# Parameter loads on ScalarE's queue, the first half of x in ten loads, and a new order of a fused S4 convolution and GEGLU kernel

## Chip, cores and metric

One core of a Trainium2 chip. The metric is device time in microseconds of one execution of the whole kernel; the table below also has the span from a profiled execution, from its first to its last instruction.

## What is computed

Two branches read the same input x (2048 tokens, 640 channels) and a gate mixes them: a causal convolution of every channel with a kernel K built from 128 complex modes, and a feed-forward layer of width 1728 with a GELU gate. Everything comes in and goes out as bfloat16.

```python
g  = sigmoid((x * gate_w).sum(-1, keepdims=True))
dt = exp(log_dt)[:, None];  logdA = dt * (A_re + 1j*A_im);  dB = dt * (B_re + 1j*B_im)
K  = einsum("dn,dnl,dn->dl", C_re + 1j*C_im, exp(logdA[:, :, None] * arange(2048)), dB).real
a  = irfft(rfft(pad(x)) * rfft(pad(K)))[:2048] + x * Dskip      # over time, per channel
b  = (gelu(x @ w_gate) * (x @ w_up)) @ w_down                    # 640 -> 1728 -> 640
out = g * a + (1 - g) * b
```

## The kernel before

The program is a set of named steps (`step(name, fn)`), each of which issues a few instructions on one engine, and a text, ORDER, that lists the names in the order in which they are emitted. Every engine runs its instructions in that order, and so does each queue of DMAs; semaphores make an instruction wait for what it reads and for what still uses the place it writes. A suffix in ORDER gives a product's PSUM tile (`/0` to `/3`) or the engine of an eviction (`/A` ScalarE, `/D` VectorE). The DMAs of SP and ScalarE share eight semaphores in turn (DMAHW0 to DMAHW7 in the rows below): a DMA is only issued when the last one with its semaphore has landed.

The work goes in stages.

- *Loads.* `lp0` to `lp5` load the six parameter arrays, `lpk` a constant with identity matrices, `ldt` the step sizes, `lw0` the first block of gate and up weights in two DMAs (line 277, 278), `x0.0` to `x4.0` the first 1024 tokens of x, one transposing DMA of 128 channels each (line 285). `t0` to `t5` turn the parameters on TensorE (line 302), `dt` is ScalarE's first exponential (line 322), `c2`, `c3` copies (331), `al`, `th`, `v0` to `v18` small vector arithmetic.
- *Tables.* For each half h of the channels, `xa`, `xb` are exponentials (ScalarE), `fb`, `fa` phase chunks (VectorE, lines 481 and 474), `qb`, `qa` the quarter turn, `sb`, `sa` sines (lines 490 and 484), `ma`, `pa`, `pb`, `pc` table products (VectorE); `pa6.h` is the last. `ct{h}.0` to `.6` then contract the tables to K on TensorE, and `ek{h}.0` to `.6` evict it. The second half's exponentials overwrite the tables, so they wait for the contraction of the first.
- *Gate and up products.* `g{ft}.{th}`, `u{ft}.{th}` multiply 128 columns of weights by 1024 tokens of half th (two blocks of 512 tokens, five matmuls each, line 381); `eg`, `eu` evict them. They stand between the table steps. `h.{th}` holds the last 64 columns of both, and is evicted in two instructions of 64 rows. Up values and the second half's gate values go through a ring of three buffers to DRAM and come back later (`su`, `sg`, `rl`, `rg`, `hm`).
- *Spectra.* `U` and `K` are matmuls with cosine and sine matrices (lines 706, 719), evicted by `eU`, `eK`. `gl` computes the gate in 80 matmuls of one column (line 625).
- *Products and output.* For half h and block c of 512 frequencies, `m{h}{c}{i}{part}` multiplies spectrum i of x with spectrum c - i of K (lines 761, 764), `s...` adds it to the sum (765), `y{h}{c}0/1` close it (767, 768), all on VectorE; `I` transforms back (779), `D` is the down projection (794, 28 matmuls each), `Z` adds the convolution through a permutation (801, 802), `o` and `st` scale, evict and store.

One buffer holds each product of `m` until its `s` has added it:

```python
step(f"m{h}{c}{i}{part}", lambda ux=ux, kx=kx: tt(out=fl(t), in0=ux, in1=kx, op=ALU.mult))
step(f"s{h}{c}{i}{part}", lambda dst=dst, op=op: tt(out=fl(dst), in0=fl(dst), in1=fl(t), op=op))
```

Of the kernel before, what the change touches and what calls it, by code (L numbers as in the profile page):

```python
# [40 lines left out]
lp0 lpk ldt idx one tdt/0 tabE dt oa.0 sk leu2 lp5 lw0 lp3 t0/1 al xb23.0 xa4.0 xb6.0 xa10.0 al2 xa5.0 xa17.0 lp4 x0.0  # L41
lp2 t4/2 t2/3 xb4.0 xa19.0 c2 xb9.0 xb14.0 x1.0 t5/0 x4.0 x3.0 lp1 t3/1 c3 x2.0 v0 v3 ur0 ob.0 xa9.0 xb17.0 xb2.0
xb1.0 xb13.0 xa1.0 xa3.0 v1 v5 v2 t1/3 ul0 th v4 xb12.0 v6 v7 xb5.0 xa8.0 xb8.0 fb0.0 fb1.0 qb0.0 g1.0/1 eg1.0/D v8
uf0.1 v11 uf0.0 u1.0/2 xb21.0 xb11.0 v9 xa16.0 xb15.0 v10 xa11.0 xb3.0 xb27.0 xa14.0 eu1.0/D g0.0/0 u0.0/3 eu0.0/A v12
v13 v14 mag xb31.0 v15 xa7.0 xb7.0 xb29.0 xb25.0 xb19.0 xb10.0 xa15.0 v16 tabT sb0.0 x4.1 lw1 qb1.0 eg0.0/D g3.0/1
# [5 lines left out]
sa1.0 eg9.0/A fa3.0 sa2.0 pa1.0 u10.0/1 eu10.0/A qa3.0 sa3.0 pa2.0 u9.0/2 eu9.0/A fa4.0 qa4.0 pa3.0 fa5.0 sa4.0 fa6.0
qa5.0 pa4.0 qa6.0 eu8.0/A g11.0/0 u12.0/1 u11.0/2 eg11.0/A sa5.0 ma5.0 fil.0 pa5.0 g10.0/3 su8.0 su9.0 lu00 lw7 leu0
h.0/0 sa6.0 pa6.0 eu12.0/A eg10.0/D ct0.4/1 ek0.4/D eu11.0/A ct0.0/2 ct0.6/3 ek0.6/D uf2.0 uf2.1 ct0.3/1 ek0.0/A
eg13.0/A ct0.2/2 ct0.1/3 ek0.1/D ek0.3/A su10.0 su12.0 su11.0 ct0.5/1 ek0.2/D ek0.5/D ur3 oa.1 ob.1 u12.1/3 tabE2
xb8.1 fil.1 eu12.1/D ks.0 xa7.1 xb29.1 xb27.1 xb9.1 xa1.1 xb13.1 ma0.1 xa8.1 xb3.1 xa9.1 xa10.1 xb4.1 xa14.1 xb19.1
# [5 lines left out]
fb4.1 pc2.1 qb4.1 U002/0 eU002/A sb3.1 eg2.1/A sb4.1 u4.1/1 U001/0 eU001/A eu4.1/A su2.1 lfm3 g4.1/2 eg4.1/A pc3.1
fb5.1 pb3.1 fa0.1 pc4.1 qb5.1 qa0.1 pb4.1 lw11 sg2.1 lka2 kt.0 sg4.1 eu3.1/A sb5.1 lka0 su4.1 su3.1 u5.1/0 U003/1
eU003/A fa1.1 pb5.1 qa1.1 sa0.1 eu5.1/A sa1.1 g5.1/2 g7.1/3 K002/1 g6.1/0 fa2.1 pa0.1 qa2.1 eg5.1/A fa3.1 pa1.1 qa3.1
sa2.1 eg6.1/A sa3.1 pa2.1 fa4.1 fa5.1 qa4.1 qa5.1 pa3.1 u6.1/2 gl/0 lw12 lfm0 sg5.1 su5.1 lka1 sg6.1 eu6.1/A su6.1
eK002/A lwd0 rl0.0 U000/2 eU000/D eg7.1/A sa4.1 u7.1/3 K003/2 fa6.1 pa4.1 qa6.1 sa5.1 gl1 eu7.1/A eK003/A sa6.1 K001/0
# [812 lines left out]
```

## Time and profile before

| | |
|---|---|
| time, median of 3 runs | 290.39 us (289.47, 290.39, 292.72) |
| profiled execution, span | 287.8 us; no other time of it is given |
| busy, PE / VectorE / ScalarE | 264.4 / 261.7 / 221.0 us |
| DMA | 46.94 MB, mean 163 GB/s |

Durations below are from the profiled execution. Busy time of an engine leaves out register, semaphore and DMA-issuing instructions; overlapping instructions of one engine are counted once, and a group's mean is that of one instruction from its issue to its end, so that two back to back take less than twice the mean. DVE is VectorE, ACT ScalarE, PE TensorE, PEld its weight loads; SPq and ACTq are the DMA issues on the queues of SP and ScalarE. The digits of PEclk are the clock granted to TensorE in 40 equal slices, in tenths of full speed.

### The profile page before, as it was taken

How to read it: one execution, taken by the hardware profiler on the slowest of the kernel's cores; microseconds unless marked ns; L12 is line 12 of the kernel's file. 1: busy time of each engine (PE TensorE's matmuls, PEld its weight loads, DVE VectorE, ACT ScalarE, POOL GpSimd, SP SyncE). 2: the span in 40 equal slices, each digit the busy share in tenths (PEclk: the TensorE clock that was granted, in tenths of full speed). 3: DMA queues.
4: the chain of work that ended last, by engine and by line, in shares of the span. 5: the costliest groups of instructions: out<-in, count | busy, mean ns of one | idle time of the engine just before them, and what ended most of it. 6: DMA issues, size and time to landing. Idle time of an engine off the chain costs nothing.

```text
span 287.8 us, 4927 instructions
## 1 busy us (share of the span) xinstructions
PE 264.4 (92%) x1869; PEld 159.4 (55%) x1883; DVE 261.7 (91%) x339; ACT 221.0 (77%) x321; POOL 16.0 (6%) x23
## 2 busy tenths in 40 slices
PE   3599999999999797997899999999997999999994
PEld 1544444444844343463674456777775667777763
DVE  1399999999899999999799998999999999999971
ACT  4799999999779999998999799897976443624120
POOL 1302060000020000000000010000000000000000
PEclk9979999999999999995999999999999999999999
DMA  8986487993668797898828669835392000000201
GB/s 207 207 224 193 132 298 178 211 236 118 182 224 202 200 308 227 226 272 259 234 76 223 206 193 294 235 80 179 109 284 73 2 23 23 25 23 2 68 23 46
DMA packets 64300, 46.94 MB, mean 163 GB/s; under 512 B 23403, under 2 KB 54166, under 8 KB 64278
## 3 DMA queue, kind: packets, MB, share of 16 engines
q1 hardware_dynamic: 63318, 44.90, 55.8%
q0 software_dynamic: 384, 1.31, 1.7%
...
## 4 chain that ended last, share of the span: by engine, by line
DVE 47%; PE 30%; DMA 7%; issue 6%; ACT 4%; SPq 4%; POOL 0%; DVEq 0%; ACTq 0%
PE ps L381 25%; DVE work L764 11%; DVE work L765 11%; DVE work L761 8%; DMA work<-Ud 2%; DVE H L695 2%; SPq L285 2%; DVE work L388 2%; DVE work L767 2%; DMA xT<-in_A_u_dram 2%; DMA early<-in_A_u_dram,back 2%; DVE work L695 2%; DVE work L768 2%; ACT tail L490 1%; PE ps L794 1%
## 5 line engine op out<-in xcount | busy, mean ns | idle before, releaser
L381 PE MATMUL ps<-xT,Wr 128*128 128x512 bf16 x526 | 120.9, 386 | 6.5 <-ACT work L386 2.3
L381 PEld LDWEIGHTS <-Wr 128*128 128x128 bf16 x540 | 53.4, 99 | 70.9 <-issue 8.8
L386 ACT CAST work<-ps 128x640 bf16<-128x640 f32 (+1 forms) x59 | 47.8, 839 | 24.8 <-PE ps L779 15.7
L765 DVE TENSOR_TENSOR work<-work 128x2560 bf16<-128x2560 bf16 x24 | 35.7, 1487 | 0.5
L794 PE MATMUL ps<-xT,work 128*128 128x320 bf16 x224 | 31.7, 299 | 0.0
L794 PE MATMUL ps<-xT,H 128*128 128x320 bf16 x224 | 31.4, 299 | 0.0
L794 PEld LDWEIGHTS <-H 128*128 128x128 bf16 x224 | 21.9, 98 | 8.5
L794 PEld LDWEIGHTS <-work 128*128 128x128 bf16 x224 | 21.9, 98 | 8.5
L484 ACT ACTIVATE tail<-work 128x1920 bf16<-128x1920 int16 x14 | 25.2, 1816 | 0.5 <-DVE work L469 0.4
L508 DVE TENSOR_TENSOR work<-tail,work 128x1920 bf16<-128x1920 bf16 (+1 forms) x22 | 23.8, 1093 | 0.5 <-ACT tail L490 0.5
L392 ACT ACTIVATE Wr<-ps,gs 128x320 bf16<-128x320 f32 x28 | 13.2, 526 | 13.1 <-issue 9.5
L779 PE MATMUL ps<-work,tail 128*128 128x320 bf16 x128 | 19.7, 299 | 3.0 <-DVE work L767 3.0
L490 ACT ACTIVATE tail<-work 128x960 bf16<-128x960 int16 (+1 forms) x24 | 20.7, 927 | 0.0
L474 DVE SCALAR_TENSOR_TENSOR work<-tail 128x320 int32<-128x320 f32 x42 | 17.9, 483 | 0.5 <-ACT tail L484 0.5
L779 PEld LDWEIGHTS <-tail 128*128 128x128 bf16 x128 | 12.3, 98 | 9.0 <-DVE work L767 4.0
L706 PEld LDWEIGHTS <-early 128*128 128x128 bf16 x128 | 12.4, 98 | 7.0 <-issue 1.4
L469 DVE TENSOR_SCALAR work<-work 128x960 int32<-128x960 int16 (+1 forms) x26 | 16.1, 627 | 0.1
L499 DVE TENSOR_TENSOR work<-tail,work 128x1920 bf16<-128x1920 bf16 x14 | 15.9, 1150 | 0.0
L719 PE MATMUL ps<-KTt,early 128*128 128x320 bf16 x80 | 15.5, 313 | 0.5 <-ACT early L392 0.3
L365 POOL DMA_INDIRECT early<-in_A_u_dram,back x8 | 11.0, 1371 | 67.3 <-DVE early L372 57.0
L392 ACT ACTIVATE work<-ps 128x640 bf16<-128x640 f32 x15 | 10.4, 714 | 5.3 <-PE ps L719 5.2
L462 ACT ACTIVATE work<-tail 128x320 bf16<-128x320 f32 x30 | 12.5, 456 | 2.0 <-DVE tail L324 2.0
(120 smaller groups left out, 411.8 us busy)
## 6 DMA issues: line engine op xcount, KB each, us to landing
...
```

Of the source, the lines that this page charges most:

```text
L381: P.matmul(t[:, x, :], lhsT=Wr[:, slot, kt, cols:cols + 128], rhs=xT[:, th, kt, 512 * x:512 * x + 512], start=(kt == 0), stop=(kt == 4))
L386: A.copy(out=out, in_=in_)
L392: act(out=out, in_=in_, func=ACT.Copy, scale=scale)
L474: stt(out=t[:, 0, x], in0=at["th"][:, d], scalar=float(A_OF[3 * c + x] + MID), in1=at["ph45"][:, d], op0=ALU.mult, op1=ALU.add)
L484: act(out=T, in_=low16(t)[:, :, :, ::2], func=ACT.Sin, scale=SIN_SCALE)
L490: act(out=o[:, r], in_=i[:, r], func=ACT.Sin, scale=SIN_SCALE)
L508: tt(out=B2[:, :, :, cols].rearrange("p r g x -> p g r x"), in0=Tv if hf == 0 else Tv[:, :, ::-1], in1=e, op=ALU.mult)
L761: step(f"m{h}{c}{i}{part}", lambda dst=dst, ux=ux, kx=kx: tt(out=fl(dst), in0=ux, in1=kx, op=ALU.mult))
L764: step(f"m{h}{c}{i}{part}", lambda ux=ux, kx=kx: tt(out=fl(t), in0=ux, in1=kx, op=ALU.mult))
L765: step(f"s{h}{c}{i}{part}", lambda dst=dst, op=op: tt(out=fl(dst), in0=fl(dst), in1=fl(t), op=op))
L779: P.matmul(t[:, r, 0:W2], lhsT=IM[:, e, m, r], rhs=Y[:, r, m], start=(m == 0), stop=(m == 3))
L794: P.matmul(t[:, x, 0:W2], lhsT=H[c // 2][:, ft, tk:tk + 128], rhs=at[f"Wd{h}"][:, ft], start=(ft == 0), stop=False)
```

## The change

The loads of the parameters and of the first weight block go from SP's queue to ScalarE's. x's first half comes in ten transposing loads of 128 channels by 512 tokens (`x0.0a`, `x0.0b`, ...), and the first four products are split into one step per block of 512 tokens (`g0.0` and `g0.0b`, ...). Beside this: the sines of a `b` chunk are one instruction, and its interleaving is done by `phase_b`, which writes runs of four; `ek` evicts two PSUM banks in one instruction; `h.th` is evicted in one instruction of 128 rows (`e13.th`); a second buffer t1 takes the products of part 1; ring buffers are handed out in the order of use; a mixing matrix `perm` takes two scalings for three; `th`, the second half's K and the inverse matrix IM lie elsewhere in SBUF; and ORDER is written anew.

```diff
     for i in range(6):
-        step(f"lp{i}", lambda i=i: (A if i == 0 else S).dma_start(out=at["prm"][:, i],
-                                                                 in_=PRM[i].rearrange("(p j) n -> p (j n)", p=128)))
+        step(f"lp{i}", lambda i=i: A.dma_start(out=at["prm"][:, i], in_=PRM[i].rearrange("(p j) n -> p (j n)", p=128)))
...
-    step("lw0", lambda: load_w(0, 0))
+    step("lw0", lambda: load_w(0, 0, A))
     for kt in range(5):
-        step(f"x{kt}.0", lambda kt=kt: load_x(kt, 0))
+        for x in range(2):
+            step(f"x{kt}.0{'ab'[x]}", lambda kt=kt, x=x: load_x(kt, 0, 512 * x, 512 * x + 512))
...
-    def gu(job, slot, cols, th):
+    def gu(job, slot, cols, th, xs=(0, 1)):
         t = PS[bank[job]]
-        for x in range(2):
+        for x in xs:
...
+                if n:
+                    step(j, lambda j=j, n=n, f=f, th=th: gu(j, n % 2, 128 * f, th), j, True)
+                else:
+                    step(j, lambda j=j, f=f: gu(j, 0, 128 * f, 0, (0,)), j, True)
+                    step(j + "b", lambda j=j, f=f: gu(j, 0, 128 * f, 0, (1,)))
...
+                        step("e13.0", lambda eng="A", j=j: copy(eng, halves(H[0][:, 13]), PS[bank[j]][:]))
+                        step("su13.0", lambda: S.dma_start(out=Ud[0][0:64, 13], in_=H[0][64:128, 13]))
...
-            ts(out=t[:, 0, x], in0=at["th"][:, d], scalar1=8.0 * (3 * c + 1 + x), scalar2=TURN / 8, op0=ALU.mult, op1=ALU.add)
+            o = t[:, 0, 0:n].rearrange("p x d -> p (x d)").rearrange("p (g x w) -> p x g w", x=n, w=4)[:, x]
+            ts(out=o, in0=at["th"][:, d].rearrange("p (g w) -> p g w", w=4), scalar1=8.0 * (3 * c + 1 + x), scalar2=TURN / 8,
+               op0=ALU.mult, op1=ALU.add)
...
-        for r in range(2):
-            act(out=o[:, r], in_=i[:, r], func=ACT.Sin, scale=SIN_SCALE)
+        act(out=T[:, :, 0:n], in_=low16(t[:, :, 0:n])[:, :, :, ::2], func=ACT.Sin, scale=SIN_SCALE)
...
-            for b in range(nb):
-                copy(eng, dst[:, b], src[:, b])
+            copy(eng, dst, src)
...
-            Pt, X, t = at["P"][:, c % 2], at["X"], at["t"]
+            Pt, X, tb = at["P"][:, c % 2], at["X"], (at["t"], at["t1"])
...
-                    dst = (Pt, X)[part]
+                    dst, t = (Pt, X)[part], tb[part]
...
-m1301 s1301 y130 y131 Z101 D110/0 D111/2 Z111 st100 o101/A st101 o111/A Z110 I120/1 I121/3 eI121/A eI120/A D120/2
-o110/A st110 st111 Z120 o120/A st120 D121/3 Z121 o121/D D130/1 I130/0 eI130/A I131/2 Z130 o1301/A o1300/A eI131/D
-D131/3 Z131 o1310/D st121 st1300 st1301 st1310 o1311/D st1311
+D111/1 Z120 Z121 o120/A Z111 m1320 s1320 m1330 s1330 m1300 m1331 s1331 m1301 s1301 st110 st120 D131/3 o111/A D130/1 st111
+o121/A st121 s1300 y131 y130 I130/0 I131/2 eI130/A Z130 o1301/D eI131/A o1300/A st1300 st1301 Z131 o1310/A st1310 o1311/D
+st1311
```

The start of ScalarE before: two DMAs, the first table load, dt, and then exponentials of `xb` and `xa` (each row is an instruction with the tiles written and read; `early` holds the parameters, what stands in brackets is waited for):

```order
L270 DMA early<-in_A_A_re_dram 128x640
L265 DMA picks<-picks_c 128x400
L321 ACT_TABLE_LOAD
L322 ACTIVATE early<-ps_63 128x640 [waits PE_49]
L462 ACTIVATE work<-tail 128x80x4 [waits DVE_49]
```

The same place after the change:

```order
L265 DMA picks<-picks_c 128x400
L270 DMA early<-in_A_C_im_dram 128x640
L270 DMA early<-in_A_A_re_dram 128x640
L270 DMA early<-in_A_C_re_dram 128x640
L270 DMA early<-in_A_B_re_dram 128x640 [waits DMAHW1_49]
L270 DMA early<-in_A_B_im_dram 128x640 [waits DMAHW3_49]
L276 DMA Wr<-in_B_w_gate_dram 128x5x256 [waits DMAHW5_49]
L277 DMA Wr<-in_B_w_up_dram 128x5x256 [waits DMAHW0_49]
L321 ACT_TABLE_LOAD
L322 ACTIVATE early<-ps_66 128x640 [waits PE_49]
L270 DMA early<-in_A_A_im_dram 128x640 [waits DMAHW1_49]
L331 CAST early<-ps_64 128x640 [waits PE_49]
```

Eight DMAs now stand ahead of the table load and one behind dt; DMAHW0 was last used by the fourth transposed half, x2.0a.

SP's queue after the change, from its start (L284 transposes, L361 loads x for the spectra; before, the transposes were of 128x1024 with the parameter loads between them):

```order
L266 DMA work<-in_A_log_dt_dram 1x640
L284 DMA_TRANSPOSE xT<-in_A_u_dram 128x512 x3
L284 DMA_TRANSPOSE xT<-in_A_u_dram 128x512 [waits DMAHW0_49]
L284 DMA_TRANSPOSE xT<-in_A_u_dram 128x512 [waits DMAHW2_49]
L284 DMA_TRANSPOSE xT<-in_A_u_dram 128x512 [waits DMAHW4_49]
L284 DMA_TRANSPOSE xT<-in_A_u_dram 128x512 [waits DMAHW6_49]
L284 DMA_TRANSPOSE xT<-in_A_u_dram 128x512 [waits DMAHW7_49]
L361 DMA early<-in_A_u_dram 128x2x640 [waits DMAHW2_49,DMAHW5_49,DMAHW1_49,PE_49]
L284 DMA_TRANSPOSE xT<-in_A_u_dram 128x512 [waits DMAHW3_49]
L284 DMA_TRANSPOSE xT<-in_A_u_dram 128x512 [waits DMAHW4_49]
```

Eight halves are issued ahead of the load for the spectra, which waits for TensorE's turn of the last parameter (its place in `early` is that of the parameters), and the last two behind it.

VectorE's last products before (L764 is an m, L765 an s, L767 and L768 the y steps):

```order
L764 TENSOR_TENSOR work<-work,tail 128x2560
L765 TENSOR_TENSOR work<-work 128x2560
L764 TENSOR_TENSOR work<-tail,early 128x2560
L765 TENSOR_TENSOR work<-work 128x2560
L764 TENSOR_TENSOR work<-tail,early 128x2560
L765 TENSOR_TENSOR work<-work 128x2560
L767 TENSOR_TENSOR work<-work 128x1280
L768 TENSOR_TENSOR work<-work 128x1280
```

And after (L777 is an m, L778 an s; those that write `early` use the new buffer t1):

```order
L777 TENSOR_TENSOR work<-tail,early 128x2560
L777 TENSOR_TENSOR early<-work,tail 128x2560
L778 TENSOR_TENSOR work<-work,early 128x2560
L777 TENSOR_TENSOR early<-tail,early 128x2560
L778 TENSOR_TENSOR work<-work,early 128x2560
L778 TENSOR_TENSOR work<-work 128x2560
L781 TENSOR_TENSOR work<-work 128x1280
L780 TENSOR_TENSOR work<-work 128x1280
```

Products and sums no longer alternate strictly: two products in a row, and the sum of the first of them last.

More of the change, by code (lines that the diff above doesn't have):

```diff
@@ L40 @@
 ORDER = """
[L41 to L45, printed above, removed]
@@ L51 @@
[L51 to L55, printed above, removed]
@@ L61 @@
[L61 to L65, printed above, removed]
@@ new lines @@
+sa4.0 u11.0/1 qa5.0 sa5.0 fa6.0 pa4.0 qa6.0 eu11.0/A ma5.0 fil.0 sa6.0 lw6 u10.0/0 pa5.0 su11.0 u12.0/2 pa6.0 h.0/1 eu10.0/A
+uf2.0 uf2.1 eg11.0/A e13.0/A ct0.1/0 ct0.6/3 ct0.4/1 eu12.0/A ur3 ek0.6/D lw7 ek0.4/A fb1.1 ct0.5/2 fb0.1 ct0.2/3 ek0.5/A
+ct0.0/1 lu00 us2 ct0.3/2 oa.1 ul3 su8.0 su12.0 tabE2 leu3 ek0.2/D su10.0 ek0.0/D ek0.3/D g12.0/3 ek0.1/D uf3.1 xb5.1 g12.1/2
+xa3.1 lw8 xb8.1 xb21.1 xb10.1 xb3.1 fil.1 xa19.1 xb6.1 xa8.1 xa16.1 xb1.1 xb13.1 eg12.1/D sg12.1 xa17.1 uf3.0 u12.1/0 us3
+ks.0 xa4.1 eg12.0/D eu12.1/D xa14.1 xa11.1 xa1.1 xb23.1 xa15.1 h.1/2 e13.1/D xa10.1 xb9.1 xb11.1 xb29.1 xb25.1 xb4.1 u0.1/3
@@ new lines @@
+pc4.1 sg4.1 sb5.1 su4.1 eu5.1/A lfm1 su5.1 qa0.1 fa1.1 pb5.1 qa1.1 eK002/A lka3 sa0.1 fa2.1 pa0.1 qa2.1 g6.1/1 eg6.1/A K012
+g5.1/0 sa1.1 eg5.1/A fa3.1 u6.1/1 sa2.1 eu6.1/A U002/3 pa1.1 qa3.1 fa4.1 leu0 leu1 lfm0 pa2.1 qa4.1 lka0 u7.1/0 sa3.1 fa5.1
+eK012/A su6.1 U000/2 pa3.1 eU002/A U001/1 qa5.1 K000/3 sa4.1 eK000/A K010 eu7.1/A sg6.1 fa6.1 eU000/A K003/2 pa4.1 qa6.1
+sa5.1 sa6.1 eK003/D g7.1/0 K013 lwd0 rl6.0 eK013/A pa5.1 pa6.1 ct1.3/2 su7.1 lw12 eg7.1/A ct1.0/0 eK010/D sg5.1 tabG eU001/D
+sg7.1 ek1.3/D gl2 lu01 ge7.0 ct1.1/1 ct1.2/2 ek1.0/D ek1.2/A ek1.1/D ct1.4/3 ek1.4/A rl7.0 ct1.5/0 ct1.6/1 rl0.0 m0001 m0000
@@ L185 @@
     H0 = sb.tile([128, NFT, 1024], BF16, name="H0")
-    early = sb.tile([128, 29696 // 2], BF16, name="early")
+    early = sb.tile([128, 32768 // 2], BF16, name="early")
+    tail = sb.tile([128, 16896 // 2], BF16, name="tail")
     KTt = sb.tile([128, 5, D], BF16, name="KTt")
@@ L199 @@
     work = sb.tile([128, 91904 // 2], BF16, name="work")
-    tail = sb.tile([128, 19200 // 2], BF16, name="tail")
     def place(base, at, dtype, *dims):
@@ L397, in halves, with ring @@
         return v.rearrange("p (x t) -> p x t", x=2)
-    turn_no = [0]
-    def ring():
-        turn_no[0] += 1
-        return at["ring"][:, turn_no[0] % at["ring"].shape[1]]
+    free = list(range(3))
+    held = {}
+    left = {}
+    def ring(key, uses):
+        if key not in held:
+            held[key], left[key] = free.pop(0), uses
+        slot = held[key]
+        left[key] -= 1
+        if not left[key]:
+            free.append(slot)
+        return at["ring"][:, slot]
     def spill(which, name, eng_step, src, dst, rows):
-        r = ring()
-        step(eng_step, lambda eng="A", r=r: copy(eng, halves(r[0:rows]), PS[bank[name]][src]))
-        step(f"s{which}", lambda r=r: S.dma_start(out=dst, in_=r[0:rows]))
+        step(eng_step, lambda eng="A": copy(eng, halves(ring(which, 2)[0:rows]), PS[bank[name]][src]))
+        step(f"s{which}", lambda: S.dma_start(out=dst, in_=ring(which, 2)[0:rows]))
     def gate_up(th, n0, pairs):
@@ L651, in perms @@
     def perms(c, eng):
[L652 to L655 removed]
+        for k in range(2):
+            x = 4 * c + k
+            scaled(eng, at["perm"][:, 0, c, k], ident, gs[:, 3, x + 2:x + 3])
+            scaled(eng, at["perm"][:, 1:3, c, k], picks[:, 128:384].rearrange("p (i q) -> p i q", i=2), gs[:, 4, x:x + 1])
     gate_up(1, 14 - len(LATE) // 2, [p for p in (6, 0, 1, 2, 3, 4, 5) if 2 * p in LATE])
```

127 lines of the change are left out of this document (64 added, 63 removed).

## Prediction

> **What bounds the kernel now.** I read the page's totals first, then busy time by stage, then each engine's own waits, because 90% busy on three engines at once says nothing about which of them sets the end.
>
> ```profile
> span 287.8 us, 4927 instructions
> PE 264.4 (92%) x1869; PEld 159.4 (55%) x1883; DVE 261.7 (91%) x339; ACT 221.0 (77%) x321; POOL 16.0 (6%) x23
> PEclk9979999999999999995999999999999999999999
> core 0: us, PE busy (x) PEld busy (x) DVE busy (x) ACT busy (x) POOL busy (x), PEclk, DMA share, GB/s
> 0.00:17.18 17.18, 9.00 (x66) 6.27 (x67) 6.72 (x10) 11.43 (x22) 3.85 (x11) 0.93 0.92 200
> 17.18:73.10 55.92, 55.43 (x251) 25.09 (x255) 55.56 (x94) 54.98 (x68) 7.01 (x4) 0.99 0.76 199
> 73.10:141.70 68.60, 62.09 (x483) 33.16 (x488) 64.00 (x105) 62.65 (x87) 2.91 (x5) 0.95 0.81 238
> 141.70:277.30 135.60, 131.16 (x1023) 90.29 (x1026) 132.66 (x131) 90.27 (x144) 2.20 (x3) 1.00 0.39 115
> 277.30:287.80 10.50, 6.72 (x49) 4.59 (x47) 2.76 (x6) 1.64 (x3) 0.00 (x0) 1.00 0.15 47
> ```
>
> I cut the span where the work changes: the loads until VectorE's first phase chunk (17.18); the first tables beside the first gate and up products, until VectorE ends the last table product pa6.0 (73.1); the same for the second half, until pa6.1 (141.7); the spectral products and the down projection, until the last product y131 (277.3); the tail. In the second window PE, VectorE and ScalarE are each busy for 55 of 55.9 us: whoever starts late there pays in full. In the third all three have 4.6 to 6.5 us free, so waits set it. In the fourth VectorE has 2.9 us free and PE 4.4: both are the bound.
>
> **Start and first stage: taken as no change.** Before, the parameters sit between the transposes on SP's queue, and ScalarE is free for its exponentials at once.
>
> ```profile
> 1.63 1.28 ACT L321 ACT_TABLE_LOAD   x1 [1.63 <-PEq L862]
> 3.32 0.70 ACT L322 ACTIVATE early<-ps 128x640 bf16<-128x640 f32 x1 [0.41 <-PE ps L308]
> 4.19 1.50 SPq L285 DMA_TRANSPOSE xT<-in_A_u_dram  x1
> 5.18 0.82 DVE L324 TENSOR_TENSOR tail<-ps,early 128x640 f32<-128x640 f32 x1 [5.18 <-PE ps L302]
> 6.04 0.47 ACT L462 ACTIVATE work<-tail 128x320 bf16<-128x320 f32 x1 [2.02 <-DVE tail L324]
> 10.72 0.69 ACT L331 CAST early<-ps 128x640 bf16<-128x640 f32 x1 [1.70 <-PE ps L302]
> 11.45 0.82 DVE L336 TENSOR_TENSOR work<-ps,early 128x640 f32<-128x640 f32 x1 [4.92 <-ACT early L331]
> 14.63 1.04 PE L302 MATMUL ps<-picks,early 128*128 128x64 bf16 x10 [2.38 <-DMA early<-in_A_A_im_dram]
> 11.23 5.31 DMA xT<-in_A_u_dram
> 0.74 0.38 ACTq L270 DMA_DIRECT2D early<-in_A_A_re_dram  x1
> 1.15 0.45 ACTq L265 DMA_DIRECT2D picks<-picks_c  x1
> 10.61 0.58 SPq L270 DMA_DIRECT2D early<-in_A_A_im_dram  x1
> ```
>
> Now eight DMAs stand on ScalarE's queue ahead of its first table load, and the last of them, the second half of lw0, waits until the fourth transposed half has landed (its DMA semaphore is shared with it). At 0.45 us each without a wait the eight end at 0.74 + 8 x 0.45 = 4.3. With the wait: a transpose of 1024 rows holds SP for 1.50 us, so I take 0.75 for a half; the fourth is issued at 1.1 + 3 x 0.75 = 3.4 and lands after half to two thirds of the 5.31 us of the chain's row, at some 6.5. Then 0.45 issue, 1.28 table, 0.70 dt: dt ends at **8.9** instead of 4.0. The lowest case, no wait, is 6.3; the highest, halves that cost as much as wholes (1.1 + 3 x 1.50 + 5.31 = 10.9), is 13.3. I take 8.9, since the rows of the transposes are the nearest.
>
> What this does: ScalarE's first copy (c3) starts at 9.3, behind the issue of lp1. Before, it began at 6.04 but lost 1.70 us at 10.72, so it is 9.3 - 7.7 = 1.6 late. It is given back one evicted tile less (0.95) and five pairs of sines made into one instruction each (1.90 against 1.82, 0.4 in all): the last sine sa6.0 ends 0.2 later.
>
> ```profile
> 115.31 2.85 ACT L386 CAST work<-ps 128x1024 bf16<-128x1024 f32 x3
> 99.94 1.90 ACT L490 ACTIVATE tail<-work 128x960 bf16<-128x960 int16 x2
> 119.33 1.85 ACT L484 ACTIVATE tail<-work 128x1920 bf16<-128x1920 int16 x1
> ```
>
> VectorE waited until 11.45 for the copies of c; they now come at 10.0 and 11.0, so its first phase chunk starts about 1 us earlier than 17.18, and it evicts one tile more (1.2): +0.2. PE: the first product stands behind the turn of lp1, which landed 4.0 us after its issue (10.61 to 14.6); issued at 8.9 it lands near 12.5, so the half products start near 13 instead of 15.4. They run at first at the half clock (the second and third digits of PEclk dip before too), and 250 full products are left at 20: 20 + 53.7 = 73.7 against 73.3 before. The earlier x therefore buys PE little: its half products are early, but VectorE and ScalarE, full until 73.1, set the stage. Bounds: -2.6 (dt at 6.3) to +4.4 (dt at 13.3).
>
> Here a rule speaks against the change. SP's queue is held 1.50 us by a transpose while the DMA share of the first window is 0.92. The Trainium skill, "DMA: Bandwidth & Descriptors", section "Issuing engines are not separate DMA queues", says that transfers issued by different engines run on the same 16 DMA engines and that only issue time is saved. By it, c would come no earlier than before, the 1 us of VectorE would be gone, and the stage would be 1 us longer; by the row of SP, whose issue alone takes 1.5 us a transpose, it is not. The difference is inside my range.
>
> **Unknown: the phase chunk's strided write.** phase_b now writes runs of four int32 with a gap, 30 times over both halves. No row has this form.
>
> ```profile
> L481 DVE TENSOR_SCALAR work<-tail 128x320 int32<-128x320 f32 x32 | 8.4, 319 | 0.0
> L474 DVE SCALAR_TENSOR_TENSOR work<-tail 128x320 int32<-128x320 f32 x42 | 17.9, 483 | 0.5 <-ACT tail L484 0.5
> L512 DVE TENSOR_SCALAR work<-work 128x320 bf16<-128x320 bf16 x4 | 1.0, 256 | 0.1
> ```
>
> Runs of four stand in L512 (fill_b), the same operation and size, which takes 256 ns, less than the 319 of the dense L481; were it to fall to the pace of L474 it would cost 164 ns each, 4.9 us in all, half in each table stage. I take nothing, the nearer row, and keep 4.9.
>
> **Second stage: -4.3.** Three things move. (a) VectorE's list up to pa6.1 loses eg10.0, ek0.4, ek0.5, eU000, eK001 and three evictions of 64 rows, which cost as much as whole ones; it gains ek0.0, ek0.3, eK003, eu0.1, eg1.1 and the merged e13.1:
>
> ```profile
> 96.10 1.23 DVE L388 CAST work<-ps 64x1024 bf16<-64x1024 f32 x1
> 73.11 1.22 DVE L388 CAST H<-ps 128x1024 bf16<-128x1024 f32 x1
> 144.55 2.44 DVE L388 CAST tail<-ps 128x504 bf16<-128x504 f32 x4
> 141.69 1.55 DVE L394 TENSOR_SCALAR early<-ps 128x640 bf16<-128x640 f32 x2
> ```
>
> Out: 1.2 + 2 x 1.2 + 2 x 0.75 + 3 x 1.2 = 8.7. In: 2 x 1.2 + 0.75 + 3 x 1.2 = 6.7. Net **-2.0**. A merged ek (128x1008 in one) I price like the 128x1024 row, 1.2, as the two of 504 were: nothing. (b) VectorE's one long wait goes:
>
> ```profile
> 127.76 2.14 PE L625 MATMUL ps<-gwc,xT 128*128 128x1 bf16 x80
> DVE early L394 <- ACT early L392: 2.3, 1, 2.3
> ```
>
> It waits at 136.5 for k spectra that PE makes late. The one 5 in PEclk is that place: right after the 80 one-column products of the gate, PE is at half clock. In the new order the gate product stands among the second half's exponentials, some 35 us earlier, and the spectra are spread between the products: **-2.3**, -0 if the wait only moves. The Trainium skill, "TensorE: Matmul & The Clock Gate", section "Part 1: The HAM clock gate (the "warmup" mystery)", has the clock fall after a window of 3.4 us that counts as idle. By that rule it would fall again behind the moved gate product; if VectorE waited there as long, the total would be 2.3 higher. (c) ScalarE has to get there in time. After the last sine it now does four copies, two ek and the table load, 4 x 0.95 + 2 x 1.07 + 1.28 = 7.2, without the two holes it had:
>
> ```profile
> 75.35 1.08 ACT L386 CAST early<-ps 128x504 bf16<-128x504 f32 x2 [1.55 <-PE ps L521]
> 81.47 0.74 ACT L466 ACTIVATE work<-tail 128x640 bf16<-128x640 f32 x1 [1.89 <-remote]
> ```
>
> So the exponentials begin at 72.2 + 7.2 = 79.4, not 81.5. Among the sines it copies 11 wide tiles for 14 and 8 narrow ones for 5: -2.9 + 2.0. With the merged sines it is over 3 us ahead by sa6.1 even if its waits for PE stay, and 5 without them. VectorE's 4.3 then holds to within a microsecond.
>
> **Last stage and tail: -2.1.** VectorE loses four 640-wide evictions and gains one (-2.2), gains one ek (+1.2), and runs more products without a wait on the one before it. With one buffer t each product and its sum must alternate:
>
> ```profile
> 258.96 1.48 DVE L761 TENSOR_TENSOR work<-early,work 128x2560 bf16<-128x2560 bf16 x1
> 260.36 1.48 DVE L764 TENSOR_TENSOR work<-work 128x2560 bf16<-128x2560 bf16 x1
> 261.88 1.49 DVE L765 TENSOR_TENSOR work<-work 128x2560 bf16<-128x2560 bf16 x1
> ```
>
> Start to start is 1.52 when the second needs the first (the last two rows) and 1.40 when it does not (the first two). In the order such pairs fall from 34 to 25: 9 x 0.12 = 1.1. VectorE: -2.1. Behind its last product the tail also gets shorter, because the down products D131 now stand ahead of it:
>
> ```profile
> 279.69 3.80 PE ps L794 x28
> PE ps L779 <- DVE work L767: 3.0, 3, 1.9
> ```
>
> On VectorE's account that would be -2.1 - 3.8. But PE is as full as VectorE: from 141.7 to the end it is busy 131.2 + 6.7 us, and moving D131 only fills time if PE has any. What it has is the 3.0 us of its waits for the y steps. I let 2.1 of these go, as much as VectorE gets ahead. Ends: 0 and -5.9.
>
> **Sum** against the profiled span: 0 - 4.3 - 2.1 = -6.4, so 281.4. The span lies 2.6 under the median of the three runs (290.39); with the same 2.6 around it the time is **284.0**.
>
> **Rivals.** (1) *The strided write is slow.* 30 x 0.164 = +4.9: 288.9. L474 speaks for it, L512 against. Within 1%. (2) *The change moves work but not the end*: the wait before pa6.1 comes back elsewhere and PE's waits stay, leaving -2.0: 288.4, also within 1%. For it: all engines over 90%. (3) *Slower: ScalarE's queue blocks.* If every half transpose costs what a whole one does, dt ends at 13.3 and the stage that has no free time is 4.4 longer; if the parameters, which now run beside them (DMA share 0.92), also double their landing, the fourth lands at 5.6 + 2 x 5.31 = 16.2, dt ends at 18.6 and the stage is 9.7 longer: 293.7. It turns slower than before once dt ends later than 8.9 + 6.4 = 15.3. For it: no second engine could relieve ScalarE there. Against it: before, the whole half of x came between 4.2 and 16.5 us beside parameters and weights.
>
> **How the numbers follow.** Forecast 0.60, rival 1 0.10, rival 2 0.18, rival 3 0.12. A measurement of this kernel tells about 1% (a time from 287.5 to 293.3 counts as the same) from no change. Of the forecast's own range, 279.5 to 288, nearly all is faster; with the rivals: faster 0.62, same 0.26, slower 0.12. The range reaches from 279.5 (dt early, all of PE's waits gone) to 292.5, which takes in both unknowns of start and stride one at a time.
>
> **What will show it.** dt (L322) near 8.9 and the first exponential near 10; pa6.0 near 73; the first of the second exponentials near 79.5 and pa6.1 near 137.5; phase chunks still 0.24 us apart; PE without a wait before I130 longer than 0.7 us. It is wrong if dt ends after 12, if L497 takes over 400 ns, if a half clock window lies in the last stage, or if PE waits over 6 us there.

## The result, and the profile after

Four runs of the changed kernel have a median of **287.13 us** (285.26 to 287.45), beside 290.48 us (289.47 to 292.72) for the kernel before on the same chip: a ratio of 0.9866, 95% interval [0.9818, 0.9914]. Two later measurements of the unaltered kernel gave 0.9856 [0.9755, 0.9958] and 0.9869 [0.9827, 0.9911]. So it is faster by 1.3%, some 3.9 us by the ratio and 3.4 by the medians; 6.4 were forecast. Runs more than 1.5% above the fastest of the same kernel are left out of every ratio here, and the profiled executions of e8 and e11 are such runs, so their rows in the table below weigh less.

The totals of the profile after, and under them its chain of work that ended last:

```profile
span 285.4 us, 4912 instructions
PE 262.5 (92%) x1883; PEld 159.3 (56%) x1883; DVE 256.5 (90%) x327; ACT 218.8 (77%) x299; POOL 15.0 (5%) x23
PEclk9999999999999999999899999999999999999999
PE 47%; DVE 19%; ACT 14%; DMA 11%; issue 5%; SPq 2%; ACTq 0%; DVEq 0%
```

The profiled execution took 287.2 us in all. The chain of the kernel before read as follows:

```profile
DVE 47%; PE 30%; DMA 7%; issue 6%; ACT 4%; SPq 4%; POOL 0%; DVEq 0%; ACTq 0%
```

The two have changed places: VectorE has lost 5.2 us of work, and TensorE now leads. Busy time by stage after the change, cut at the same steps as before, to within 0.2 us (first phase chunk, pa6.0, pa6.1, the last y step):

```profile
core 0: us, PE busy (x) PEld busy (x) DVE busy (x) ACT busy (x) POOL busy (x), PEclk, DMA share, GB/s
0.00:18.44 18.44, 10.53 (x75) 7.56 (x76) 6.54 (x9) 8.32 (x14) 3.24 (x9) 1.00 0.86 188
18.44:75.20 56.76, 53.74 (x248) 23.96 (x246) 56.55 (x94) 56.25 (x69) 6.39 (x6) 1.00 0.75 192
75.20:138.50 63.30, 59.82 (x489) 32.63 (x488) 61.46 (x98) 60.35 (x77) 3.78 (x5) 0.97 0.82 241
138.50:276.40 137.90, 133.78 (x1046) 92.11 (x1045) 130.73 (x126) 91.52 (x137) 1.61 (x3) 1.00 0.43 123
276.40:285.40 9.00, 4.65 (x34) 3.00 (x31) 1.25 (x3) 2.38 (x4) 0.00 (x0) 0.99 0.12 36
```

Start and first stage together are 2.1 longer than before (75.2 for 73.1), the second stage is 5.3 shorter, the stage of the products 2.3 longer, and the tail 1.5 shorter: -2.4 in all. TensorE's idle time in a row is its length less its busy time: in the five rows 7.9, 3.0, 3.5, 4.1 and 4.4, before 8.2, 0.5, 6.5, 4.4 and 3.8. The idle time saved in the second stage stands in the first one again; what TensorE gained in all is 1.9 us of busy time. Where that can come from the clock records show: before, its products ran at half clock from 15.4 to 18.3 and from 130.9 to 137.8, after only from 135.0 to 138.4. The PEclk of the first row is no evidence for it: it counts the time ahead of the first clock record (11.5 us before, 15.5 after) as full.

One profile is one execution, so the stages of all of them stand side by side. This table is worked out from the traces: end of dt, end of pa6.0, length of the second stage, of the products' stage (to the end of y), of the tail, and where the clock records have the half clock from 90 us on (the last microsecond left out).

| kernel | dt | pa6.0 | 2nd | products | tail | span | half clock |
|---|---|---|---|---|---|---|---|
| before | 4.0 | 73.2 | 68.6 | 135.5 | 10.5 | 287.8 | 130.9-137.8 |
| after | 11.8 | 75.3 | 63.3 | 138.0 | 8.9 | 285.4 | 135.0-138.4 |
| after again (e5) | 11.5 | 75.0 | 65.2 | 135.9 | 8.8 | 285.0 | none |
| after again (e10) | 12.4 | 75.9 | 65.2 | 137.6 | 8.9 | 287.6 | 137.6-141.0 |
| lw0 behind dt (e1) | 8.6 | 73.1 | 63.3 | 135.7 | 8.9 | 281.0 | none |
| lw0 behind dt (e9) | 7.9 | 74.1 | 65.2 | 138.2 | 8.9 | 286.4 | 135.8-139.2 |
| whole transposes (e2) | 9.3 | 74.0 | 64.0 | 135.1 | 8.7 | 281.8 | none |
| e1 and e2 (e11) | 5.8 | 75.1 | 65.5 | 137.3 | 8.7 | 286.5 | 136.5-140.0 |
| start freed (e8) | 4.8 | 75.3 | 65.1 | 138.6 | 8.7 | 287.6 | 136.5-139.9 |
| gate product late (e3) | 12.2 | 75.7 | 68.0 | 135.8 | 8.8 | 288.3 | 131.4-134.8 |
| D131 behind y (e4) | 12.6 | 76.1 | 63.9 | 135.9 | 11.3 | 287.3 | none |
| ring loads early (e7) | 12.4 | 75.9 | 66.0 | 136.6 | 8.8 | 287.3 | 133.4-140.2 |
| before, gate early (e6) | 4.5 | 74.5 | 74.2 | 137.0 | 10.4 | 296.1 | 95.4-102.3, 139.8-143.2, 232.0-235.4 |
| before, gate early (e12) | 4.0 | 73.7 | 72.6 | 136.6 | 10.4 | 293.3 | 96.0-99.4, 136.9-140.3, 229.1-232.5 |

**The start.** ScalarE's queue after the change, in order of time (start, duration, what), then SP's row:

```profile
5.85 0.33 ACTq L270 DMA_DIRECT2D early<-in_A_B_im_dram  x1
6.22 0.45 ACTq L276 DMA_DIRECT2D Wr<-in_B_w_gate_dram  x1
9.38 0.40 ACTq L277 DMA_DIRECT2D Wr<-in_B_w_up_dram  x1
9.81 1.28 ACT L321 ACT_TABLE_LOAD   x1 [9.81 <-DMA xT<-in_A_u_dram]
11.10 0.70 ACT L322 ACTIVATE early<-ps 128x640 bf16<-128x640 f32 x1
1.16 10.35 SPq L284 DMA_TRANSPOSE xT<-in_A_u_dram  x8
```

VectorE's and ScalarE's longest waits there (us in total, times, longest):

```profile
DVE tail L324 <- ACT early L322: 11.8, 1, 11.8
ACT L321 <- DMA xT<-in_A_u_dram: 9.8, 1, 9.8
```

Eight halves hold SP for 10.35 us, 1.29 each; 0.75 was taken. The fourth is issued at 5.02 and lands at 9.33, lw0's second half is issued right after it, and dt ends at 11.80. VectorE, which has had nothing to do until then, does al, al2, and then v1 at 13.19; from there it has no hole above 0.2 us until pa6.0.

**The phase chunk** in its strided form (min, median and max in ns):

```profile
L497 DVE TENSOR_SCALAR work<-early x32: 307/318/541, 18.4 to 112.3; 128x320 int32<-128x320 f32 x32
```

The dense form took 319. The rival of the slow strided write is out.

**The end of the second stage.** TensorE, in order of time (x10 of L381 is one gate or up product):

```profile
125.71 2.32 PE L381 MATMUL ps<-xT,Wr 128*128 128x512 bf16 x10
129.62 1.25 PE L719 MATMUL ps<-work,early 128*128 128x320 bf16 x8 [1.59 <-ACT early L392]
130.71 0.98 PE L732 MATMUL ps<-KTt,early 128*128 128x320 bf16 x6
132.50 0.43 PE L732 MATMUL ps<-KTt,early 128*128 128x320 bf16 x2 [0.82 <-ACT early L392]
134.00 0.97 PE L732 MATMUL ps<-KTt,early 128*128 128x320 bf16 x6 [1.07 <-DMA xT<-in_B_w_down_dram]
134.81 4.01 PE L381 MATMUL ps<-xT,Wr 128*128 128x512 bf16 x10
```

The same ten products take 2.32 at 125.71 and 4.01 at 134.81, 1.7 us more. In between TensorE waits three times, for ScalarE's evictions and for a load. Busy time in two stretches of 3.40 us there:

```profile
131.40:134.80 3.40, 1.52 (x11) 0.86 (x9) 3.40 (x6) 3.40 (x5) 0.00 (x0) 1.00 1.03 341
135.00:138.40 3.40, 3.40 (x9) 1.22 (x8) 3.27 (x4) 2.39 (x2) 0.00 (x0) 0.50 0.90 255
```

TensorE idles for 1.88 of 3.40 us, and in the next 3.4 its clock is 0.50. In the kernel before, the half clock stood right behind the gate product. Now there is none behind the gate product (98.9 to 100.8); it comes 34 us later, behind these waits, and stretches the last gate product g7.1, behind which k's last contraction and the next stage stand.

**The tail.** TensorE from 269.9 on:

```profile
269.86 7.77 PE L807 MATMUL ps<-xT,work 128*128 128x320 bf16 x56
277.46 2.34 PE L792 MATMUL ps<-work,tail 128*128 128x320 bf16 x16
```

I130 follows D131 and D130 without a wait, as forecast. But VectorE's last y step ended at 276.55, only 0.9 us before: it is not far ahead.

### The profile page after: what moved, and what is told of

It reads as the page before. It is cut to its first block, busy times and chain, and to the rows that moved or that the text cites. A ratio compares the mean times of both kernels' runs of the same rounds, so it can differ in the third digit from the quotient of the medians.

```text
span 285.4 us, 4912 instructions
## 1 busy us (share of the span) xinstructions
PE 262.5 (92%) x1883; PEld 159.3 (56%) x1883; DVE 256.5 (90%) x327; ACT 218.8 (77%) x299; POOL 15.0 (5%) x23
## 3 DMA queue, kind: packets, MB, share of 16 engines
q10 hardware_dynamic: 2608, 1.91, 2.9%
q0 software_dynamic: 384, 1.31, 1.6%
## 4 chain that ended last, share of the span: by engine, by line
PE 47%; DVE 19%; ACT 14%; DMA 11%; issue 5%; SPq 2%; ACTq 0%; DVEq 0%
PE ps L381 26%; PE ps L807 11%; DMA work<-Ud 6%; DVE work L778 4%; PE ps L792 3%; DVE work L774 3%; DVE work L777 3%; DVE early L777 2%; DVE work L708 2%; DMA xT<-in_B_w_down_dram 2%; ACT work L477 2%; DVE H L708 2%; DMA out_dram<-Wr 2%; ACT work L481 2%; PE ps L732 2%
## 5 line engine op out<-in xcount | busy, mean ns | idle before, releaser
L381 PE MATMUL ps<-xT,Wr 128*128 128x512 bf16 x540 | 121.4, 383 | 3.0 <-DVE work L388 1.9
L381 PEld LDWEIGHTS <-Wr 128*128 128x128 bf16 x540 | 53.0, 99 | 66.0 <-issue 6.3
L386 ACT CAST work<-ps 128x640 bf16<-128x640 f32 (+1 forms) x58 | 46.1, 826 | 17.9 <-PE ps L792 12.2
L392 ACT ACTIVATE Wr<-ps,gs 128x320 bf16<-128x320 f32 x30 | 14.2, 529 | 16.9 <-PE ps L815 11.8
L504 ACT ACTIVATE tail<-work 128x1920 bf16<-128x1920 int16 (+1 forms) x12 | 19.8, 1655 | 0.0
L489 DVE SCALAR_TENSOR_TENSOR work<-early,tail 128x320 int32<-128x320 f32 x42 | 18.0, 481 | 0.1
L778 DVE TENSOR_TENSOR work<-work,early 128x2560 bf16<-128x2560 bf16 x12 | 17.9, 1488 | 0.2
L778 DVE TENSOR_TENSOR work<-work 128x2560 bf16<-128x2560 bf16 x12 | 17.8, 1487 | 0.2
L719 PEld LDWEIGHTS <-early 128*128 128x128 bf16 x128 | 12.4, 98 | 8.1 <-issue 2.6
L792 PEld LDWEIGHTS <-tail 128*128 128x128 bf16 x128 | 12.4, 98 | 6.5 <-DMA tail<-im_c 1.1
L719 PE MATMUL ps<-work,early 128*128 128x320 bf16 x80 | 13.0, 299 | 2.0 <-ACT early L392 1.6
L477 ACT ACTIVATE work<-tail 128x320 bf16<-128x320 f32 x30 | 12.9, 457 | 0.6 <-PE ps L535 0.3
```

Of the source, the lines that this page charges most:

```text
L381: P.matmul(t[:, x, :], lhsT=Wr[:, slot, kt, cols:cols + 128], rhs=xT[:, th, kt, 512 * x:512 * x + 512], start=(kt == 0), stop=(kt == 4))
L386: A.copy(out=out, in_=in_)
L477: act(out=B2m[:, 1, :, hf, s], in_=at["al"][:, 0, d].rearrange("p (g w) -> p g w", w=4), func=ACT.Exp, scale=8.0 * m)
L489: stt(out=t[:, 0, x], in0=at["th"][:, d], scalar=float(A_OF[3 * c + x] + MID), in1=at["ph45"][:, d], op0=ALU.mult, op1=ALU.add)
L504: act(out=T[:, :, 0:n], in_=low16(t[:, :, 0:n])[:, :, :, ::2], func=ACT.Sin, scale=SIN_SCALE)
L719: P.matmul(t[:, r, 0:W2], lhsT=FM[:, m, e, r], rhs=pm[:, r, e], start=(e == 0), stop=(e == 1))
```

## The experiments

Each expectation stands as it was written before the run. A diff shows the words of ORDER that move; e1 to e12 is the order in which the kernels ran.

**1 (e1): lw0 behind dt.**

```diff
-lp4 lp5 lw0 t0/2 tabE dt lp1 c3
+lp4 lp5 t0/2 tabE dt lp1 lw0 c3
```

> After the change, with one word of the order moved: both halves of lw0 are issued by ScalarE behind dt and lp1 instead of ahead of the table load. Theory 'queue' (the 2.1 us that the first stage lost come from ScalarE standing until 9.81 behind lw0's second half, which waits for a transposed half to land): the last parameter ahead is issued at 5.85 + 0.33, so dt ends near 8.2 instead of 11.8, VectorE begins with al near 8.2 instead of 11.84, PE's idle 1.90 and 0.94 us before evictions (24.7 and 38.0) go, pa6.0 ends 2 to 3 us earlier, near 72.5 to 73, and the time falls to about 284.5 to 285. Rival 'arrival' (the stage begins with the arrival of x and of the first weights, which now are asked for 2 us later): dt early as well, but PE's first product later than 15.7 and pa6.0 at 75 or later: 287 to 289.

dt ended at 8.56, the first product began at 13.46 (15.68), pa6.0 ended at 73.1. There are only two times to compare, 283.47 and 284.53, too few for a ratio; the ninth run took it up again.

```profile
7.85 0.70 ACT L322 ACTIVATE early<-ps 128x640 bf16<-128x640 f32 x1
13.46 6.87 PE L381 MATMUL ps<-xT,Wr 128*128 128x512 bf16 x21
132.61 2.32 PE L381 MATMUL ps<-xT,Wr 128*128 128x512 bf16 x10
```

**2 (e9): the same again.**

> The first experiment's kernel again (after the change, lw0 issued behind dt and lp1), in five rounds, because only two of its runs there can be compared. Theory 'queue': the first stage again ends near 73, 2 us or more ahead of the unaltered kernel beside it, and the time is 284 to 286, 1 to 3 us under it. Rival 'arrival', or a chance of that one profile: stage of 75, time of the unaltered kernel.

pa6.0 ended at 74.1. With the six profiles whose start is that of the change (75.0 to 76.1, mean 75.7) the queue theory holds for the stage: the two with lw0 behind dt end it at 73.6, 2.0 earlier. For the time it does not: 0.9894 [0.9831, 0.9956], no better than the unaltered kernel beside it. Part of the reason shows in g7.1 (2.32 in the last row of e1), of which nine products are recorded here, and in the stretch in which they ran:

```profile
135.77 3.79 PE L381 MATMUL ps<-xT,Wr 128*128 128x512 bf16 x9
```

```profile
135.80:139.20 3.40, 3.40 (x9) 1.21 (x9) 3.27 (x4) 2.35 (x2) 0.00 (x0) 0.50 0.91 264
```

One kernel, two executions: from pa6.0 to the end it took 207.8 us without the half clock there and 212.3 with it. The half clock costs g7.1 itself 1.7 us; in all TensorE is busy 2.0 us longer and idle 2.4 us longer in the second execution, and what brought the rest is not shown.

**3 (e2): five whole transposes.**

```diff
-        step(f"x{kt}.0{'ab'[x]}", lambda kt=kt, x=x: load_x(kt, 0, 512 * x, 512 * x + 512))
+        step(f"x{kt}.0{'ab'[x]}", lambda kt=kt, x=x: None if x else load_x(kt, 0))
```

> After the change, with x's first half again in five transposes of 1024 rows (the second word of each pair does nothing); the products stay split and all other loads stay where they are. Theory 'issue' (a transpose of 512 rows holds SP's queue for 1.29 us, nearly as long as one of 1024 rows, so ten halves ask SP for twice the time): SP is done with the five by about 8 instead of 18.8, all of x's first half is there earlier, and the stage is no longer than after the change: pa6.0 at 74 to 75, time 286 to 287. Rival 'halves pay' (they give PE its first products earlier): PE's first product later than 15.7 by 1 us or more, pa6.0 later by 1 to 2, time 288 to 289. ScalarE still has lw0 ahead of its table load, behind whatever transpose shares its semaphore: dt between 9 and 12 in both.

Ratio 0.9845 [0.9785, 0.9905]; pa6.0 at 74.0. The theory's result came out, but not its way. Transposes of after, then of this run (min, median, max in ns; one of the six is of the second half):

```profile
L284 SPq DMA_TRANSPOSE xT<-in_A_u_dram x10: 1142/1258/1270, 1.2 to 17.6; - x10
```

```profile
L284 SPq DMA_TRANSPOSE xT<-in_A_u_dram x6: 1260/2360/4499, 1.2 to 18.4; - x6
```

And SP's row of the five:

```profile
1.15 13.19 SPq L284 DMA_TRANSPOSE xT<-in_A_u_dram  x5
```

A whole costs 1.26 only while nothing is in its way, later up to 4.5; five wholes held SP as long as ten halves would (13.19). That dt came at 9.3, because lw0 waits for another transfer there, is the likely reason for the shorter stage; it was not tested by itself. The first product came at 16.6, 0.9 later than after the change, and TensorE then had no hole above 0.25 us in that stage: in these two profiles the halves give it its first product earlier, and it loses that in holes.

**4 (e11): both.**

> After the change, with lw0 behind dt and lp1 and with five transposes of 1024 rows for x's first half. Theory 'arrival of the parameters' (whole transposes fill the queues: with them lp5 landed 7 us after its issue, at 10.35, where halves let it land 2.6 us after, at 8.78): dt early, near 5.5, but the parameters no earlier than with halves, VectorE's v1 at 11 to 12 and pa6.0 near 74, so the kernel is no better than with halves and lw0 behind dt. Rival 'dt decides the stage': pa6.0 at 71 to 72, time 282 to 284.

dt ended at 5.8, yet pa6.0 at 75.1; ratio 0.9876 [0.9833, 0.9919]. dt alone does not decide the stage. ScalarE's next step, the copy c3, shows why here:

```profile
11.86 0.69 ACT L331 CAST early<-ps 128x640 bf16<-128x640 f32 x1 [6.04 <-issue]
```

TensorE had made what c3 copies by 5.3, but lw0 now stood between dt and c3 in ScalarE's queue and was issued at 10.72, when the second whole transpose, which shares its semaphore, had landed; v1 needs the copy and began at 12.58. So the queue still blocked ScalarE, one step later. An order with lw0 behind c3 as well was not run.

**5 (e8): the start freed in three points.**

```diff
-lp0 lp2 lp4 lp5 lw0 t0/2 tabE dt
+lp0 lp2 tabE dt lp4 lp5 lw0 t0/2
-    step("lw0", lambda: load_w(0, 0, A))
+    step("lw0", lambda: load_w(0, 0, S))
```

with the whole transposes of e2 besides.

> After the change, with the start loosened in three points: lw0 on SP's queue ahead of the transposes, five transposes of 1024 rows in place of ten, and the table load and dt on ScalarE ahead of lp4, lp5 and lp1. Theory 'queue': dt ends near 4.6, VectorE begins with al near 4.7 and after a wait for lp4 and lp5 with the copies of c goes on near 9.5; ScalarE's exponentials begin near 5.5; the first products of PE wait for x, 12 to 14; pa6.0 near 72, the time 283 or below, no worse than with lw0 behind dt alone. Rival 'PE sets the stage once ScalarE is free': pa6.0 stays at 73 to 74 as with lw0 behind dt alone, however early dt is, because PE's products begin no earlier than 13.5 and run without a hole from there.

dt ended at 4.8, but VectorE began at 8.05 and v1 at 12.94; ratio 0.9803 [0.9701, 0.9904], not to be told from the others. VectorE's waits, and then TensorE's turns of the parameters in order of time:

```profile
DVE tail L324 <- PE ps L302: 8.1, 1, 8.1
DVE work L337 <- PE ps L302: 3.5, 1, 3.5
```

```profile
10.52 2.31 PE L302 MATMUL ps<-picks,early 128*128 128x64 bf16 x20 [2.58 <-DMA early<-in_A_C_re_dram]
13.85 2.31 PE L302 MATMUL ps<-picks,early 128*128 128x64 bf16 x20 [1.01 <-DMA early<-in_A_B_im_dram]
```

Neither theory: the parameters themselves came late. By the trace's packets lp5 landed 7.2 us after its issue (5.69 to 12.9) behind whole transposes and weights, against 2.6 us (6.19 to 8.8) in e1, where only halves were on the way; in e2, with whole transposes ahead and the weights behind it, it was 7.2 us too (3.20 to 10.35). The Trainium skill, "DMA: Bandwidth & Descriptors", section "Issuing engines are not separate DMA queues", says that another engine's queue saves issue time and not transfer time; these landings agree. Of the starts that were run e1's is the best for the stage, by single profiles: parameters and halves first, weights behind.

**6 (e3): the gate product late.**

```diff
-xa9.1 gl/0 ma5.1 ... qb3.1 pc2.1 U003/3 gl1 fb4.1
+xa9.1 ma5.1 ... qb3.1 pc2.1 U003/3 fb4.1
-eu6.1/A U002/3 ... eK012/A su6.1 U000/2
+eu6.1/A gl/1 U002/3 ... eK012/A su6.1 gl1 U000/2
```

> After the change, with the gate product (80 one-column products) put back behind the eviction of u6.1, where it stood before, some 22 us later, and its copy behind it. Theory 'gate' (its place among the spectra is what brought the half clock and VectorE's wait of 2.3 us before pa6.1): a half clock window of 3.4 to 6.8 us right behind it, the k spectra late, VectorE waiting 2 us or more for eK003, pa6.1 later by about 2.3, mean granted clock near 0.985 instead of 0.994, time near 289.5. Rival 'list' (the second stage got shorter because VectorE evicts less there, wherever the gate product stands): pa6.1 within 0.5 us of 138.5 and the time within 1 of 287.

Ratio 0.9973 [0.9938, 1.0008], some 3 us over the unaltered kernel (0.9866, its interval ends at 0.9914); the second stage took 68.0. TensorE at that place in order of time, then two stretches of it, then VectorE's longest wait there:

```profile
128.43 2.14 PE L638 MATMUL ps<-gwc,xT 128*128 128x1 bf16 x80 [2.00 <-ACT work L386]
130.97 4.01 PE L381 MATMUL ps<-xT,Wr 128*128 128x512 bf16 x10
```

```profile
128.00:131.40 3.40, 2.97 (x86) 2.58 (x86) 3.40 (x8) 3.01 (x5) 0.00 (x0) 1.00 0.61 171
131.40:134.80 3.40, 3.40 (x9) 1.22 (x8) 3.40 (x7) 2.17 (x2) 0.00 (x0) 0.50 1.08 336
```

```profile
DVE early L394 <- issue: 3.6, 1, 3.6
```

The half clock stands right behind the gate product, although TensorE counts as busy there for 2.97 of 3.40 us; the next product takes 4.01, and VectorE's wait before pa6.1 is back with 3.6. The gate theory holds: in the new order its place is worth most of the second stage's gain.

**7 and 8 (e6, e12): the kernel before, with the gate product early.**

```diff
+sg0.1 lw9 gl/0 eu13.1/D ... ma1.1 ma3.1 gl1 eg13.1/D
```

> The kernel BEFORE the change, with one thing of the change alone: the gate product and its copy stand 35 us earlier, among the second half's exponentials. Theory 'gate': this alone takes most of what the second stage gained; no half clock behind 127, VectorE's wait of 2.3 at 136.5 below 0.5, the stage 64 to 66 instead of 68.6, the time 2.5 to 4 under the kernel before, near 287. Rival 'list': without the moved evictions VectorE and ScalarE still end the stage as late; 68 or more, time within 1 of 290.5.

```diff
+g12.1/1 gl/0 eg12.1/D ... xb7.1 gl1 xb10.1
```

> The kernel BEFORE the change, with the gate product earlier once more, now in a place where its bank is free: behind g12.1 among the second half's exponentials, its copy on ScalarE between two of them. In the sixth run PE stood 3.4 us ahead of the gate product for that bank. Theory 'gate': PE loses nothing there, VectorE's 2.3 us at 136.5 go, no half clock after 127, the second stage 65 to 67 instead of 68.6, time 287 to 289. Rival 'the order made for it': in the old order the product delays the evictions' products wherever it stands, and the stage is 68 or longer, time 290 or more.

Both were slower than the kernel before, 1.023 [1.0129, 1.0331] and 1.0181 [1.0131, 1.0231]. TensorE's waits (L622 and, in the second, L626 are gate product and copy):

```profile
PE ps L622 <- DVE work L385: 3.4, 1, 3.4
```

```profile
PE ps L378 <- ACT gb L626: 2.5, 1, 2.5
```

In the old order the product waits for a bank, or the next product waits for its copy; VectorE starves behind it (4.5 us in the second), and the half clock follows. They do not measure the gate product's place alone: moving it pays only with evictions ordered for it, as the change has them.

**9 (e4): D131 behind y.**

```diff
-st110 st120 D131/3 o111/A D130/1 ... st1301 Z131
+st110 st120 o111/A D130/1 ... st1301 D131/3 Z131
```

> After the change, with the down product D131 (56 products, 7.6 us) back behind I130 and I131, as it stood before. Theory 'PE is the bound at the end' (VectorE's last sums are done early enough only because PE is late): without D131 ahead PE comes to I130 at 270.0 and waits until VectorE's y130 ends at 276.5, 6.5 us, and the 7.6 us of D131 follow behind: the time grows by about 6.5 to 293.5. Rival 'VectorE has time to spare' (the y steps would not be waited for): PE's wait below 3 us as in the kernel before, the time within 1 to 2 us of 287.

TensorE in the tail:

```profile
270.54 3.96 PE L807 MATMUL ps<-xT,work 128*128 128x320 bf16 x28 [1.08 <-ACT Wr L392]
276.05 2.33 PE L792 MATMUL ps<-work,tail 128*128 128x320 bf16 x16 [1.54 <-DVE work L780]
```

It waited 1.5 us for the y step, not 6.5, and 1.1 us for an eviction before D130: D131 has 28 products, not the 56 that the expectation counted. The tail took 11.3 instead of 8.9, the ratio was 0.9972 [0.9923, 1.0021], some 3 us over the unaltered kernel. D131 ahead of y is worth about 2.5 us. Undoing the gate product's place (e3) or that of D131 (e4) each takes away most of the whole gain.

**10 (e7): ring loads early.**

```diff
+ks.1 hm7.0 hm6.0 U011/2 ... gl3 kd.1 rl8.0 rl12.0 m0100
```

> After the change, with VectorE's product hm6.0 right behind hm7.0 (it frees a slot of the ring) and the loads rl8.0 and rl12.0 issued right behind kd.1, some 5 us earlier than before, so that VectorE's longest wait in the products' stage (2.4 us at hm12.0, for rl12.0) goes. Theory 'PE is the bound of the last stage' (from 222 on the chain of work that ended last is on PE; PE's idle there is 4.1 us, none of it at that place): VectorE's wait falls below 0.5, and the time stays within 0.7 of the unaltered kernel beside it. Rival 'VectorE is the bound of the last stage': y130 ends 2 us or more earlier and so does the kernel.

VectorE's waits for these loads fell from 3.2 us after the change and 2.4 in e10 to 1.1, and the products' stage took 136.6 (135.9 to 138.0 unaltered); ratio 0.9828 [0.9718, 0.9939]. No gain is shown, as the theory of TensorE as the bound has it, but TensorE waited 2.2 us at 163.4 for another load (0.7 us after the change), probably because the loads moved ahead delayed it, so the rival is not excluded either.

**11 and 12 (e5, e10): the unaltered kernel.**

> The kernel after the change once more, unaltered, beside the three that follow, since times of one kernel spread by 1 to 2% here. All theories expect the stages of the first profile: about 75.3 until pa6.0, 63.3 until pa6.1, 138 until y130, 9 behind it, and 286 to 288 in all. If a stage comes out more than 1 us off, that much is not to be read out of any other single profile.

> The kernel after the change, unaltered, in five rounds beside the others: 75 to 76 until pa6.0, 63 to 66 until pa6.1, 144 to 147 from there to the end; 286 to 288.

The stages vary by 0.9, 2.0 and 2.0 us between three executions of one kernel. A stage's gain below 2 us is not to be read out of one profile.

## Why the prediction was right, and where its sizes were not

The sign was right, and so was the largest term, that of the second stage. The terms of the start and of the last stage failed, and the time was 3.1 us too low: 287.13 lies nearer to the second rival (288.4) than to the forecast (284.0).

- **Start and first stage, 0: measured +2.1** (75.2 to 73.1). The step that failed is "I take 0.75 for a half": a half took 1.29, as long as a whole. So the fourth was issued at 5.02 instead of 3.4. It also took 4.3 us to land, where 3.1 were taken, and landed at 9.33 instead of 6.5. dt ended at 11.8 instead of 8.9, inside the bounds given (12.4 in e10), and v1 began at 13.19 instead of 10.5, 1.74 later than before. VectorE's list behind v1 grew by 0.39, where 1.2 were forecast; the two make the 2.1. Moving lw0 alone takes 2.0 of it away in the stage (e1, e9). TensorE's first product, forecast at 13, came at 15.68, no earlier than before (15.43), and two holes of 1.90 and 0.94 us before evictions followed.
- **Strided write, 0: right**, 318 ns.
- **Second stage, -4.3: measured -5.3**, in the other two profiles -3.4 each: -4.0 on average. VectorE's list fell by 2.5 (64.00 to 61.46; 1.9 in the other two profiles; -2.0 was forecast), and its wait of 2.3 went. That this hangs on the gate product e3 shows. The exponentials began at 81.8 instead of 79.4, because the stage ahead was late, and 7.7 us after the last sine, where 7.2 were counted.
- **Last stage and tail, -2.1: measured +0.8**, and 0.0 on average of three profiles (137.2 + 8.8 against 135.5 + 10.5). This is the larger miss. VectorE did get less work, 135.4 to 132.0, and D131 is worth 2.5. The step that failed is "I let 2.1 of these go": the 3.0 us for which TensorE waited for the y steps did go, but on average it got no less idle, since other waits came in their place. Its waits from 138.5 to 276.4 after the change:

```profile
PE ps L732 <- ACT Wr L392: 1.0, 1, 1.0
PE ps L732 <- ACT tail L386: 0.9, 1, 0.9
PE ps L534 <- ACT early L392: 0.8, 1, 0.8
PE ps L792 <- DMA tail<-im_c: 0.7, 1, 0.7
PE ps L719 <- DVE work L453: 0.5, 1, 0.5
```

They are for ScalarE's evictions, a load and VectorE, not for y. From pa6.1 to the end TensorE was busy 137.9 us and idle 8.2 before, and 138.4 and 8.5 after (137.5 and 7.3 in e5, 137.8 and 8.6 in e10). It leads the chain there, so VectorE's shorter list bought next to nothing.
- **The half clock is a smaller part of it.** The prediction let it go with the gate product; it weighed only a return right behind the moved one. It came back behind TensorE's waits for the k spectra, in six of ten profiles of the changed order (e3, whose gate product stands elsewhere, left out). It costs g7.1 1.7 us. Second and products' stage together took 201.2 to 203.7 with it (mean 202.7) and 199.0 to 201.2 without (e1, e2, e4, e5; mean 199.8), but these are different kernels; in the unaltered one they took 201.2 and 202.8 with it and 201.2 without. The times bear this out: of the eleven runs of the unaltered kernel that count, five have a mean granted clock of 0.996 or more, less than one cell of 3.41 us at half, and a mean span of 284.7 us; the six with less have 285.4. So even without a whole cell at half the span is 3.3 over the 281.4 of the forecast. No run could place the half clock at will.
- **What decides whether it comes** the traces show. In each of them all changes of the clock lie on one grid of 3.41 us, and the grid's place differs from execution to execution. The waits before g7.1 sum to 3.48 us after the change (1.59 + 0.82 + 1.07) and to 3.47 in e1; but the largest share that falls into one cell of the grid is 1.88 after the change and 1.21 in e1, where it is cut by the cells' ends. In the six with half clock there this share is 1.88 to 2.12, in the four without 1.21, 1.76, 1.80 and 1.91. So about 1.9 us of 3.41 is the point from which the next cell runs at half. It is no sharp one: e5 has 1.91 without it, and so have two cells of the kernel before, with 1.88 and 1.89.
- **Rivals.** "ScalarE's queue blocks" was half right: dt at 11.8 cost 2.1 and not 4.4. "Moves work, not the end" names what happened to the last stage, where TensorE's waits stayed, and not to the second.

This bears on a rule. The Trainium skill, "TensorE: Matmul & The Clock Gate", section "Part 1: The HAM clock gate (the "warmup" mystery)", has an activity window of 3413 ns that runs freely and does not start with the kernel. The trace agrees, by the grid above. The section has the clock fall after a window that was idle; here 1.9 of 3.41 us were enough, and in e3 0.5 us of waits beside the 2.1 us of the gate product.
